# Attention with block gating and a Fourier-mixing MLP on one core: from the ninth head pair on, DMAs that transpose turn q, k and the gate mask, in place of TensorE

## The chip, the core and the metric

The kernel runs on one core of a Trainium2 chip. Its engines work side by side and meet through semaphores: TensorE (PE, matrix products and transposes by matmul, results to PSUM), VectorE (DVE), ScalarE (ACT), GpSimd (POOL) and SyncE (SP, which here issues DMAs). The metric is the device time of one execution in microseconds (us).

## The reference, cut to what matters

Inputs: q, k and v of 4 batches, 8 heads, 768 positions and 64 dimensions in float32, and two weight matrices of 512 x 2048 and 2048 x 512. First comes attention in which each query sees only some blocks of 64 keys:

```python
k_rep = k.reshape(B, H, n_blocks, block, D).mean(axis=3)      # 12 blocks of 64 keys
gate = einsum('bhsd,bhnd->bhsn', q, k_rep)                    # causal: later blocks at -1e9
sel  = top 3 blocks by gate, and the query's own block
scores = 0.125 * q @ k.T, kept where the block is selected and key <= query
attn = softmax(scores) @ v
```

Then, per batch, with x of 768 x 512 (the 8 heads side by side): `mixed = real(fft over rows and columns of x)`, `u = x + mixed`, `un = normalise(u)` along a row, `out = u + relu(un @ w_ch1) @ w_ch2`.

The gates choose blocks by comparison, so they are computed more finely than one f16 product would: in f32 for the first eight head pairs, and from f16 high and low parts for the rest.

## The kernel before, in words

Heads go in pairs, kk = 0 to 15, four per batch; the two heads of a pair are e = 0 and 1. A pair's q and k are loaded in natural layout (128 positions per partition group, six groups) as float32 (load_qk, line 211, by SP, four pairs ahead of use) into tiles of two buffers.

- stage_A (line 264) turns k (who = 1) and q (who = 0) by twelve f32 transposes on TensorE into PSUM tile `tp`. Out of `tp` for k, VectorE sums 64 keys at a time (`kr12`, line 292) and ScalarE writes f16 kI (line 311); for q, from pair SPLIT = 8 on, ScalarE writes the f16 high part `qh` scaled by 64 (line 287) and VectorE the low part `ql` (line 288), and VectorE makes high and low parts of the block sums, `krx` (lines 304 and 305). POOL copies q to its place in `qg` (cast_q, line 237).
- stage_B (line 316) makes the gates: ten matmuls on TensorE (line 323 in f32 for pairs below 8, line 331 in f16 from pair 8), then on VectorE the causal part (line 333), the sum with the low part (line 334), ten MAX8 (line 340), the comparison with the third largest (line 342) and the own block (line 348).
- stage_C (line 350) turns that mask by five f16 transposes (tile `gt`, line 354), and VectorE copies it to rows 64 to 75 of `qg` (line 357). Rows 64 to 75 of kI hold a constant of -60000 per block, so that one matmul of 76 rows gives scores and mask together.
- stage_S (line 376) makes a third of the scores of one head (PSUM tile `sc`, two buffers) and ScalarE their Exp into `ptl` (line 391); stage_AV (line 399) multiplies by v and normalises; fold (line 428 on) begins the Fourier part of the batch.

The order on PE and POOL is that in which the program emits instructions (manual_schedule, line 660); a scheduler orders the other engines. Each pair kk is a loop over six sections p = 0 to 5, and each section emits one stage_S, a piece of filler, one of the other stages, and filler again. The table USUAL places k of pair kk+2 at p = 0, stage_AV of the last pair's head 1 at p = 1, q of pair kk+2 at p = 2, stage_C of pair kk+1 at p = 3, stage_AV of head 0 at p = 4 and stage_B of pair kk+2 at p = 5; pair 6 (NORM_SLOT), in which the first batch's normalisation falls, has a table of its own. The filler is MLP work (stage_M1, line 578 for its matmuls; stage_M2, line 592) and Fourier work (stage_S1, stage_S2, stage_T) of batches whose attention is done, from a planner (class Feed) that hands out work by written-down costs: main(stage, cost) adds a stage's cost to its clock. After pair 15 the rest of the filler runs alone.

Of the kernel before, what the change touches and what calls it, by code (L numbers as in the profile page):

```python
# [19 lines left out]
def _consts_np():  # L20
# [30 lines left out]
    IndN = np.where(nn[:, None] == (s[None, :] // 64), NEG, 0.0).astype(np.float16)  # L51
    return dict(CS=CS, SS=SS, CD=CD, SDN=SDN, SDP=SDP, ident32=ident32, ident16=ident16,
                ut01=ut01, ltri=ltri, cz24=cz24, oth24=oth24, IndN=IndN)
# [65 lines left out]
def kernel(  # L119
# [65 lines left out]
    kI_t = [[const([128, S], F16, f"kI_{e}_{sl}") for sl in range(3)] for e in range(2)]  # L185
    v16_t = [const([128, 2, NST, 66], F16, f"v16_{sl}") for sl in range(4)]
    qg_t = [[const([128, S], F16, f"qg_{e}_{sl}") for sl in range(3)] for e in range(2)]
    warm = const([128, 512], F16, "warm")
    kr24_t = [const([128, 2 * NB], FP, f"kr24_{sl}") for sl in range(2)]
    krx_t = [const([128, 2, 2 * NB], F16, f"krx_{sl}") for sl in range(2)]  # L190
# [8 lines left out]
    NORM_SLOT = 6  # L199

# [32 lines left out]
    def cast_v(kk):  # L233
        P[kk]["v16"] = v16_t[kk % 4]
        nc.gpsimd.tensor_copy(out=v16_t[kk % 4][:, :, :, 0:64], in_=P[kk]["vn"])

    def cast_q(kk):
        d = P[kk]
        for e in range(2):
            nc.gpsimd.tensor_copy(out=d["qg"][e][0:64, :],  # L240
                                  in_=d["qt" if kk < SPLIT else "qh"][64 * e:64 * e + 64, :])
# [22 lines left out]
    def stage_A(kk, who, g):  # L264
        d = P[kk]
        src = d["qn"] if who == 0 else d["kn"]
        if who == 0 and g == 0:
            d["qt"] = apool.tile([128, S], FP, tag="qT32", name=f"qT32_{kk}")
            if kk >= SPLIT:
                parts = d["qt"].bitcast(F16)  # L270
                d["qh"], d["ql"] = parts[:, 0:S], parts[:, S:2 * S]
            d["qg"] = [qg_t[e][kk % 3] for e in range(2)]
        if who == 1 and g == 0:
            d["kI"] = [kI_t[e][kk % 3] for e in range(2)]
            d["kr12"] = spool.tile([128, NB], FP, tag="kr12", name=f"kr12_{kk}", bufs=2)
            d["kr24"] = kr24_t[kk % 2]
# [6 lines left out]
        if who == 0:  # L283
            if kk < SPLIT:
                (nc.scalar.copy if kk == LATE else nc.vector.tensor_copy)(out=d["qt"][:, cols], in_=flat)
            else:
                nc.scalar.activation(out=d["qh"][:, cols], in_=flat, func=AF.Copy, scale=QS)  # L287
                STT(out=d["ql"][:, cols], in0=flat, scalar=QS, in1=d["qh"][:, cols], op0=MULT, op1=SUB)  # L288
            if g == 1 and kk != LATE:
                cast_q(kk)  # L290
        else:
# [3 lines left out]
            if g == 1 and kk < SPLIT:  # L295
# [3 lines left out]
            elif g == 1:  # L299
                d["krx"] = krx_t[kk % 2]  # L300
                for e in range(2):
                    r, c = slice(64 * e, 64 * e + 64), slice(NB * e, NB * (e + 1))
                    hi, lo = d["krx"][r, 0, c], d["krx"][r, 1, c]
                    nc.vector.tensor_scalar(out=hi, in0=d["kr12"][r, :], scalar1=QS, scalar2=None, op0=MULT)
                    STT(out=lo, in0=d["kr12"][r, :], scalar=QS, in1=hi, op0=MULT, op1=SUB)
            for e in range(2):
                dst, src_ = d["kI"][e][0:64, cols], flat[64 * e:64 * e + 64]
                if kk < EARLY and g == 1 and e == 1:
                    nc.vector.tensor_copy(out=dst, in_=src_)
                else:  # L310
                    nc.scalar.copy(out=dst, in_=src_)  # L311

# [3 lines left out]
    def stage_B(kk):  # L316
# [9 lines left out]
        else:  # L326
            gps = pst([128, NG, 2, 2 * NB], f"g_{kk}")
            krx = d["krx"].rearrange("p o n -> p (o n)")
            for st in range(1, NST):
                for n, part in enumerate((d["qh"], d["ql"])):  # L330
                    nc.tensor.matmul(gps[:, st - 1, :, :].rearrange("p o n -> p (o n)"),
                                     part[:, 128 * st:128 * (st + 1)], krx, start=(n == 0), stop=(n == 1))
            nc.vector.tensor_tensor(out=gsf, in0=gps[:, :, 0, :], in1=cz24[:, 1:NST, :], op=ADD)
            nc.vector.tensor_tensor(out=gsf, in0=gps[:, :, 1, :], in1=gsf, op=ADD)
# [12 lines left out]
        else:  # L347
            STT(out=gm, in0=gm, scalar=QS, in1=oth24[:, 1:NST, :, :], op0=MULT, op1=MULT)

    def stage_C(kk):  # L350
# [5 lines left out]
        for e in range(2):  # L356
            nc.vector.tensor_copy(out=d["qg"][e][64:64 + NB, 128:S],
                                  in_=gt[32 * e:32 * e + NB].rearrange("p a c -> p (a c)"))
# [17 lines left out]
    def stage_S(kk, e, s):  # L376
        d = P[kk]
        if s == 0:
            d.setdefault("pt", {})[e] = apool.tile([128, 3 * SEC], F16, tag=f"ptl{e}",
                                                   name=f"ptl_{kk}_{e}")  # L380
# [3 lines left out]
        for (jt, a0, a1, co) in SECS[s]:  # L384
            diag = by_pe and a0 == 128 * jt
            nc.tensor.matmul(sp[:, co:co + (a1 - a0)],  # L386
                             d["kI"][e][0:76, 128 * jt:128 * (jt + 1)],
                             d["qg"][e][0:76, a0:a1], start=True, stop=not diag)
            if diag:
                nc.tensor.matmul(sp[:, co:co + 128], id16, ltri, start=False, stop=True)  # L390
        nc.scalar.activation(out=pt[:, SEC * s:SEC * (s + 1)], in_=sp[:, 0:SEC], func=AF.Exp,  # L391
                             scale=0.125 if kk < SPLIT else 0.125 / QS)
# [267 lines left out]
    with tc.manual_schedule(engines={mybir.EngineType.PE, mybir.EngineType.Pool}):  # L660
# [12 lines left out]
        for t in krx_t:  # L673
            nc.gpsimd.memset(t, 0.0)
        for t in gmp_t:
            nc.vector.memset(t, 0.0)
        for sl in range(3):
            for e in range(2):
                nc.gpsimd.dma_start(kI_t[e][sl][64:64 + NB, :], dr["IndN"].ap())
        nc.gpsimd.dma_start(ut01, dr["ut01"].ap())  # L680
        for e in range(2):
            for sl in range(3):
                nc.gpsimd.memset(qg_t[e][sl][64:64 + NB, 0:128], 0.0)
        load_v(0)
        for sl in range(4):
# [43 lines left out]
        for kk in range(NK):  # L729
            at = NORM if kk == NORM_SLOT else USUAL  # L730
            for p in range(6):
# [9 lines left out]
                if p == 1 and kk - 1 == NORM_SLOT:  # L741
                    main(stage_B, 0.35, kk + 1)
                if p == at["A1"] and kk + 2 < NK:
                    main(stage_AA, 0.7, kk + 2, 1)
# [66 lines left out]
```

## Time and profile before

| What | Value |
|---|---|
| Median of 3 runs | 333.61 us (332.26 to 334.58) |
| The profiled execution's own time | 332.94 us |
| Its span in the trace | 331.2 us, 7008 instructions |
| TensorE busy, matmuls / weight loads | 311.9 us / 202.9 us |
| VectorE, ScalarE, POOL busy | 235.7, 180.3, 84.7 us |
| Mean granted TensorE clock | 0.995 |
| Pair 8's first scores in the trace | about 106 us |
| Pair 15's last scores | about 249 us |

How to read it: matmuls are pipelined, so that a TensorE row's length overlaps the next one's, and the distance from start to start is what an item takes from TensorE. PEld is the weight load, which runs beside matmuls. Idle time of an engine matters only where the chain that ends last goes through it.

### The profile page before, as it was taken

Reading aid. Unit: us, or ns where it says so; the run is one execution under the profiler, and the core shown is the slowest. Engines: PE = TensorE matmul, PEld = TensorE weight load, DVE = VectorE, ACT = ScalarE, POOL = GpSimd, SP = SyncE. Lnnn points to the kernel's source line nnn. Section 1 sums busy time; section 2 is a strip of 40 time slices with the busy share of each in tenths; the row PEclk is TensorE's granted clock in tenths of the full one; section 3 lists DMA queues with packets and bytes.
Section 4 is the critical chain, followed back from the end, with each engine's and each line's share of the span. In section 5 each row is a group of like instructions: output and inputs, shape, how many; then the busy total and the mean of one; then the engine's idle time right before and its main releaser. Section 6 shows DMA issues by size and latency. Waiting matters only on the chain.

```text
span 331.2 us, 7008 instructions
## 1 busy us (share of the span) xinstructions
PE 311.9 (94%) x2712; PEld 202.9 (61%) x2712; DVE 235.7 (71%) x750; ACT 180.3 (54%) x276; POOL 84.7 (26%) x137
## 2 busy tenths in 40 slices
PE   8799998997889989998999989999999999999995
PEld 3567776876656666555666666656666654556442
DVE  3778889689776898999765898998457588433211
ACT  3188889789965855428486754535764302244000
POOL 8545573352481120504032030502030000000000
PEclk9999999998999999999999999999999999999999
DMA  8997999990799242425324000010000011100021
GB/s 203 230 256 186 246 136 226 155 221 7 165 188 181 54 96 75 103 70 136 99 48 97 2 0 35 32 65 32 34 2 0 2 64 63 65 1 2 32 95 63
DMA packets 85312, 31.18 MB, mean 94 GB/s; under 512 B 77736, under 2 KB 81136, under 8 KB 85280
## 3 DMA queue, kind: packets, MB, share of 16 engines
q1 hardware_dynamic: 79984, 25.88, 31.4%
q0 software_dynamic: 3552, 4.40, 8.5%
q10 hardware_dynamic: 1744, 0.46, 0.6%
q8 instruction: 21, 0.34, 0.4%
q14 instruction: 11, 0.09, 0.1%
HBM read 28.63 MB, written 6.29 MB: 105 GB/s over the span
## 4 chain that ended last, share of the span: by engine, by line
PE 73%; DVE 16%; ACT 7%; issue 1%; POOL 1%; DVEq 0%; ACTq 0%
PE ch L592 22%; PE ha L578 14%; PE sc L386 8%; PE hb L578 7%; PE av L412 5%; ACT kI L311 4%; PE g L323 3%; PE za L480 2%; DVE mx L340 2%; DVE ptl L397 2%; ACT ptl L391 2%; PE tp L279 2%; PE warm L365 2%; PE gt L354 2%; PE mx L507 2%; PE mx L508 2%
## 5 line engine op out<-in xcount | busy, mean ns | idle before, releaser
L391 ACT ACTIVATE ptl<-sc 128x896 f16<-128x896 f32 x96 | 87.3, 919 | 45.9 <-PE sc L386 36.6
L592 PE MATMUL ch<-w_sb,hT 128*128 128x512 f16 x384 | 91.4, 379 | 0.5 <-DVE qT L288 0.5
L578 PEld LDWEIGHTS <-w_sb 128*128 128x128 f16 x512 | 48.8, 97 | 38.6 <-issue 4.7
L578 PE MATMUL ha<-unT,w_sb 128*128 128x512 f16 x256 | 65.7, 378 | 1.8 <-DVE hT L583 1.4
L386 PE MATMUL sc<-qg,kI 76*128 76x512 f16 (+3 forms) x256 | 54.8, 306 | 3.6 <-ACT ptl L391 3.6
L592 PEld LDWEIGHTS <-hT 128*128 128x128 f16 x384 | 36.2, 97 | 35.1 <-issue 0.6
L581 ACT ACTIVATE hT<-ha 128x512 f16<-128x512 f32 x64 | 38.1, 597 | 33.5 <-PE ha L578 33.4
L583 DVE TENSOR_SCALAR hT<-hb 128x256 f16<-128x256 f32 x64 | 26.8, 421 | 28.9 <-PE hb L578 28.7
L578 PE MATMUL hb<-unT,w_sb 128*128 128x256 f16 x256 | 38.4, 272 | 1.1 <-ACT hT L581 0.7
L429 POOL TENSOR_TENSOR fs<-x 128x384 f16<-128x384 f16 x12 | 10.9, 909 | 105.5 <-DVE x L418 91.8
L386 PEld LDWEIGHTS <-kI 76*128 76x128 f16 x256 | 24.0, 100 | 20.3 <-issue 2.8
L311 ACT CAST kI<-tp 64x384 f16<-64x384 f32 x57 | 27.1, 475 | 14.6 <-DVE kr L292 13.6
L595 DVE TENSOR_TENSOR u<-ch,u 128x512 f32<-128x512 f32 x24 | 16.5, 685 | 19.9 <-PE ch L592 19.6
L412 PE MATMUL av<-v,ptl 128*128 128x65 f16 x672 | 26.2, 195 | 0.0
L412 PEld LDWEIGHTS <-ptl 128*128 128x128 f16 x672 | 24.8, 98 | 2.0
L292 DVE TENSOR_REDUCE kr<-tp 128x6 f32<-128x384 f32 x32 | 17.2, 551 | 7.0 <-PE tp L279 7.0
L397 DVE TENSOR_TENSOR ptl<-ptl,ut 128x384 f16<-128x384 f16 x36 | 16.0, 479 | 6.1 <-ACT ptl L391 5.7
L553 ACT ACTIVATE x<-u,nmr,rstd 128x512 f16<-128x512 f32 x12 | 8.9, 806 | 17.7 <-DVE nmr L546 17.6
L418 DVE TENSOR_TENSOR x<-av,rcp 128x384 f16<-128x384 f32 x32 | 17.8, 557 | 0.9
L390 PE MATMUL sc<-ltri,id 128*128 128x128 f16 x84 | 18.4, 219 | 0.0
L240 POOL COPY qg<-qT 64x768 f16<-64x768 f16 x16 | 14.4, 902 | 12.1 <-ACT qT L287 11.6
L520 DVE BATCH_NORM_STATS2 bst<-u 128x6 f32<-128x512 f32 x24 | 16.6, 692 | 1.2 <-ACT u L516 0.7
(112 smaller groups left out, 422.9 us busy)
## 6 DMA issues: line engine op xcount, KB each, us to landing
vn<-in_v_dram SPq DMA_DIRECT2D x32, 192.0 KB, 3.3
out_dram<-u SPq DMA_DIRECT2D x24, 256.0 KB, 2.0
kn<-in_k_dram SPq DMA_DIRECT2D x30, 192.0 KB, 3.3
qn<-in_q_dram SPq DMA_DIRECT2D x30, 192.0 KB, 3.4
w_sb<-in_moe_w_ch_dram POOLq DMA_DIRECT2D x8, 256.0 KB, 7.0
w_sb<-in_moe_w_ch_dram POOLq DMA_DIRECT2D x4, 512.0 KB, 9.5
cs_sb<-c_CS SPq DMA_DIRECT2D x1, 289.5 KB, 4.9
ss_sb<-c_SS SPq DMA_DIRECT2D x1, 289.5 KB, 5.2
```

Source lines behind the costliest of these rows:

```text
L292: nc.vector.tensor_reduce(out=d["kr12"][:, 6 * g:6 * g + 6], in_=ps.rearrange("p a (x c) -> p a x c", x=2), axis=mybir.AxisListType.X, op=ADD)
L311: nc.scalar.copy(out=dst, in_=src_)
L386: nc.tensor.matmul(sp[:, co:co + (a1 - a0)], d["kI"][e][0:76, 128 * jt:128 * (jt + 1)], d["qg"][e][0:76, a0:a1], start=True, stop=not diag)
L390: nc.tensor.matmul(sp[:, co:co + 128], id16, ltri, start=False, stop=True)
L391: nc.scalar.activation(out=pt[:, SEC * s:SEC * (s + 1)], in_=sp[:, 0:SEC], func=AF.Exp, scale=0.125 if kk < SPLIT else 0.125 / QS)
L397: nc.vector.tensor_tensor(out=dg, in0=dg, in1=um, op=MULT)
L412: nc.tensor.matmul(av[:, st, 0:65], pt[:, o:o + 128], d["v16"][:, e, jt, 0:65], start=(cnt == 0), stop=(cnt == 20))
L418: nc.vector.tensor_tensor(out=x_b[:, :, 64 * h:64 * h + 64], in0=av[:, :, 0:64], in1=rcp.to_broadcast([128, NST, 64]), op=MULT)
L578: nc.tensor.matmul(hp_, w1_sb[:, dt, 128 * it:128 * (it + 1)], unT[:, dt, c0:c1], start=(dt == 0), stop=(dt == NDT - 1))
L581: nc.scalar.activation(out=hT[:, c0:c1], in_=hp_, func=AF.Relu)
L583: nc.vector.tensor_scalar(out=hT[:, c0:c1], in0=hp_, scalar1=0.0, scalar2=None, op0=mybir.AluOpType.max)
L592: nc.tensor.matmul(cps, x["hT"][it][:, 128 * st:128 * (st + 1)], w2_sb[:, it, :], start=(it == 0), stop=(it == NIT - 1))
```

## The change

For pairs 8 to 15 stage_A and stage_C are not called. In their place `split` makes f16 high and low parts of q in natural layout (ScalarE and VectorE), side by side in `qs`, and of k in `ks` (high) and `klo` (low); transposing DMAs on SP's queue turn `qs` to `qhl` and `ks` to kI. `ks` has the -60000 constants in columns 64 to 75, so that they come along. `stage_R` adds up k's blocks on TensorE: 24 matmuls of two columns, with the high and low parts as stationary operand and a matrix of ones and zeros. Its result is split to f16 high and low parts on VectorE and copied to the upper partitions by ScalarE. stage_B multiplies `qhl` (high and low parts on 128 rows) by that, per head, writes the mask back into `qs` and a third DMA turns `qs` into `qg`. Each turn is 128 x 1536 f16. For all pairs, kI and `qg` hold the two heads in alternating blocks of 128 columns, `ptl` has one buffer per head in place of two, and `v16` three slots in place of four.

```diff
-    kI_t = [[const([128, S], F16, f"kI_{e}_{sl}") for sl in range(3)] for e in range(2)]
-    v16_t = [const([128, 2, NST, 66], F16, f"v16_{sl}") for sl in range(4)]
-    qg_t = [[const([128, S], F16, f"qg_{e}_{sl}") for sl in range(3)] for e in range(2)]
+    kI_t = [const([128, NST, 2, 128], F16, f"kI_{sl}") for sl in range(3)]
+    v16_t = [const([128, 2, NST, 66], F16, f"v16_{sl}") for sl in range(3)]
+    qg_t = [const([128, NST, 2, 128], F16, f"qg_{sl}") for sl in range(3)]
+    ks = const([128, NST, 2, 128], F16, "ks")
+    klo = const([128, NST, 2, 64], F16, "klo")
+    qs_t = [const([128, NST, 2, 128], F16, f"qs_{sl}") for sl in range(2)]
+    krs_t = [const([128, 2, 2, NB], F16, f"krs_{sl}") for sl in range(2)]
+    ind2 = const([128, 2], F16, "ind2")
...
+    def turn(dst, src):
+        nc.sync.dma_start_transpose(dst.rearrange("p s e c -> p (s e) c"),
+                                    src.rearrange("p s e c -> p (s e c)"))
+
+    def split(kk):
+        d = P[kk]
+        kn, qn = d["kn"], d["qn"]
+        d["qs"] = qs = qs_t[kk % 2]
+        d["qhl"] = apool.tile([128, S], FP, tag="qT32", name=f"qhl_{kk}").bitcast(F16).rearrange(
+            "p (s e c) -> p s e c", e=2, c=128)
+        khi, qhi = ks[:, :, :, 0:64], qs[:, :, :, 0:64]
+        nc.scalar.activation(out=qhi, in_=qn, func=AF.Copy, scale=QS)
+        STT(out=qs[:, 1:NST, :, 64:128], in0=qn[:, 1:NST, :, :], scalar=QS, in1=qhi[:, 1:NST, :, :],
+            op0=MULT, op1=SUB)
+        turn(d["qhl"], qs)
+        nc.scalar.activation(out=khi, in_=kn, func=AF.Copy, scale=QS)
+        turn(kI_t[kk % 3], ks)
+        STT(out=klo, in0=kn, scalar=QS, in1=khi, op0=MULT, op1=SUB)
+        d["kI"], d["qg"] = kI_t[kk % 3], qg_t[kk % 3]
+
+    def stage_R(kk):
+        d = P[kk]
+        d["krs"] = krs = krs_t[kk % 2]
+        rps = pst([64, 2, NB], f"r_{kk}")
+        for st in range(NST):
+            for e in range(2):
+                o = rps[:, e, 2 * st:2 * st + 2]
+                nc.tensor.matmul(o, ks[:, st, e, 0:64], ind2, start=True, stop=False)
+                nc.tensor.matmul(o, klo[:, st, e, :], ind2, start=False, stop=True)
+        hi, lo = krs[0:64, :, 0, :], krs[0:64, :, 1, :]
+        nc.vector.tensor_copy(out=hi, in_=rps)
+        nc.vector.tensor_tensor(out=lo, in0=rps, in1=hi, op=SUB)
+        nc.scalar.copy(out=krs[64:128, :, :, :], in_=krs[0:64, :, :, :])
...
             for st in range(1, NST):
-                for n, part in enumerate((d["qh"], d["ql"])):
-                    nc.tensor.matmul(gps[:, st - 1, :, :].rearrange("p o n -> p (o n)"),
-                                     part[:, 128 * st:128 * (st + 1)], krx, start=(n == 0), stop=(n == 1))
+                for e in range(2):
+                    nc.tensor.matmul(gps[:, st - 1, e, :, :].rearrange("p o n -> p (o n)"),
+                                     d["qhl"][:, st, e, :],
+                                     d["krs"][:, e, :, :].rearrange("p o n -> p (o n)"), start=True, stop=True)
...
-            STT(out=gm, in0=gm, scalar=QS, in1=oth24[:, 1:NST, :, :], op0=MULT, op1=MULT)
+            STT(out=d["qs"][:, 1:NST, :, 64:64 + NB], in0=gm,
+                scalar=QS * QS, in1=oth24[:, 1:NST, :, :], op0=MULT, op1=MULT)
+            turn(qg_t[kk % 3], d["qs"])
...
             d.setdefault("pt", {})[e] = apool.tile([128, 3 * SEC], F16, tag=f"ptl{e}",
-                                                   name=f"ptl_{kk}_{e}")
+                                                   name=f"ptl_{kk}_{e}", bufs=1)
...
-                             d["kI"][e][0:76, 128 * jt:128 * (jt + 1)],
-                             d["qg"][e][0:76, a0:a1], start=True, stop=not diag)
+                             d["kI"][0:76, jt, e, :],
+                             d["qg"][0:76, a0 // 128:a1 // 128, e, :], start=True, stop=not diag)
...
-                if p == 1 and kk - 1 == NORM_SLOT:
-                    main(stage_B, 0.35, kk + 1)
+                if p == 0 and kk - 1 == NORM_SLOT:
+                    main(stage_R, 0.4, kk + 1)
+                    main(stage_B, 0.3, kk + 1)
                 if p == at["A1"] and kk + 2 < NK:
-                    main(stage_AA, 0.7, kk + 2, 1)
-                if p == at["C"] and kk + 1 < NK:
+                    if kk + 2 < SPLIT:
+                        main(stage_AA, 0.7, kk + 2, 1)
+                    else:
+                        split(kk + 2)
+                if p == at["C"] and kk + 1 < min(SPLIT, NK):
                     main(stage_C, 0.3, kk + 1)
...
-                        main(stage_AA, 0.7, kk + 2, 0)
+                        if kk + 2 < SPLIT:
+                            main(stage_AA, 0.7, kk + 2, 0)
...
-                    main(stage_B, 1.05 if kk + 2 < SPLIT else 0.35, kk + 2)
+                    if kk + 2 >= SPLIT:
+                        main(stage_R, 0.4, kk + 2)
+                    main(stage_B, 1.05 if kk + 2 < SPLIT else 0.3, kk + 2)
...
+            if kk == 3:
+                nc.gpsimd.memset(ks[:, :, :, 64 + NB:128], 0.0)
+                for t in qs_t:
+                    nc.gpsimd.memset(t[:, 0, :, 64:128], 0.0)
+                for e in range(2):
+                    nc.sync.dma_start(ks[:, :, e, 64:64 + NB],
+                                      dr["IndT"].ap().rearrange("(st p) n -> p st n", p=128))
+                    nc.gpsimd.memset(ind2[:, e:e + 1], 0.0)
+                    nc.gpsimd.memset(ind2[64 * e:64 * e + 64, e:e + 1], 1.0)
...
-                pool_after(P[kk + 2]["qt" if kk + 2 < SPLIT else "ql"])
+                pool_after(P[kk + 2]["qt"] if kk + 2 < SPLIT else P[kk + 2]["kn"][:, 0, 0, :])
```

Since q and k are both scaled by 64 now, the Exp of these pairs has the scale 0.125 / 64^2.

## The prediction

> **What bounds the kernel now.** I read the page's busy shares first, then the busy time by stretches, then the timeline of the stretch that the change touches, then groups by line.
>
> ```profile
> PE 311.9 (94%) x2712; PEld 202.9 (61%) x2712; DVE 235.7 (71%) x750; ACT 180.3 (54%) x276; POOL 84.7 (26%) x137
> ...
> q1 hardware_dynamic: 79984, 25.88, 31.4%
> ...
> kn<-in_k_dram SPq DMA_DIRECT2D x30, 192.0 KB, 3.3
> w_sb<-in_moe_w_ch_dram POOLq DMA_DIRECT2D x8, 256.0 KB, 7.0
> ```
>
> TensorE (PE) is busy 94% of the span. The stretches (busy us of PE, weight loads, VectorE, ScalarE, POOL, then granted clock) say where:
>
> ```profile
> 170.00:190.00 20.00, 19.81 (x173) 12.95 (x172) 13.70 (x48) 14.48 (x23) 5.42 (x8) 1.00 0.18 41
> 190.00:210.00 20.00, 18.91 (x174) 12.61 (x172) 18.10 (x53) 10.93 (x18) 3.38 (x6) 1.00 0.04 14
> 210.00:230.00 20.00, 20.00 (x170) 11.68 (x167) 18.96 (x60) 9.91 (x13) 6.11 (x7) 1.00 0.14 53
> ```
>
> From 85 us on, where pairs 8 to 15 are prepared among the filler (MLP and Fourier work), PE hardly stops: between 125 and 250 us its waits add up to 2.8 us, all for VectorE. So PE time taken out there comes off the end, and a PE wait put in there goes onto it. VectorE is close behind (18.96 of 20 us), ScalarE is not. DMA is nearly idle (shares 0.04 to 0.45).
>
> ```profile
> 71.73 1.19 PE L323 MATMUL g<-kr,qT 128*128 128x24 f32 x10
> 72.77 0.27 PE L507 MATMUL mx<-cd_sb,yR 128*128 128x256 f16 x1
> ...
> 201.35 0.41 PE L331 MATMUL g<-krx,qT 128*128 128x48 f16 x10
> 201.61 0.27 PE L507 MATMUL mx<-cd_sb,yT 128*128 128x256 f16 x1
> ...
> 202.79 0.27 DVE L333 TENSOR_TENSOR gsb<-g,cz 128x120 f32<-128x120 f32 x1
> ...
> 204.15 0.82 PE L279 MATMUL tp<-id,kn 128*128 128x128 f32 x6
> 204.81 0.27 PE L507 MATMUL mx<-cd_sb,yT 128*128 128x256 f16 x1
> ...
> 213.83 0.46 PE L354 MATMUL gt<-id,gmp 128*44 128x128 f16 x5
> 214.22 0.28 PE L507 MATMUL mx<-cd_sb,yR 128*128 128x256 f16 x1
> ```
>
> Start to start is what an item costs PE, since ends overlap: six transposes of k 0.66 us (204.15 to 204.81), the mask's five 0.39 us, the ten f16 gate matmuls 0.26 us, ten f32 ones 1.04 us. And VectorE answers late: the gates end at 201.35 + 0.41 = 201.76, their first reader starts at 202.79, 1.0 us later.
>
> **What leaves PE**, per pair, eight pairs: twelve f32 transposes (0.66 for k, 0.65 for q, 210.54 to 211.19) and the mask's transposes (0.39, and some 0.09 of gap ahead: the matmul before starts at 213.53 and spaces 0.21). That is 0.66 + 0.65 + 0.48 = 1.79 us, times 8 = 14.3 us. The gate matmuls stay ten, with half the columns: taken as equal.
>
> **What PE gets: stage_R.** 24 matmuls of 2 columns, each with a weight load of 128 rows by 64 f16 columns. No row has that. Below: the f16 gates' full-width loads pass at 0.26 / 10 = 26 ns. Above: the f32 gates stream only 24 columns and still need 104 ns per 128-column load, so half the columns at that pace is 52 ns. The mask's 44-column loads (78 ns each with 128 columns streamed, where full-width f16 transposes, `unt`, take 57) lean to the slow side: I take 52 ns, 24 x 0.052 = 1.25 us per pair, 10.0 in all; at 26 ns 5.0, at 78 ns 15.0. [...]
>
> **The wait that this puts in.** stage_R and stage_B are written one right after the other with no filler between, and PE's order is the written one. B's first matmul needs krs, which takes three hand-overs after R's last matmul: VectorE copies the f16 part out of PSUM, VectorE subtracts, ScalarE copies to partitions 64 to 127. Floor: 0.18 us drain (an L331 matmul's own length), 0.04 to VectorE (av ends 199.41, L417 starts 199.45), 2 x 0.17 (the krx ops of the same size, L304 and L305's 152 to 168 ns), 0.03 to ScalarE (222.99 + 0.17, L553 starts at 223.19), 0.21 for 48 columns (L391 and L287: 0.84 ns per column over 0.17) and as little again back to PE: 0.8 us. On top come the queues: VectorE answered PE after 1.0, 0.8 (gates), 1.0 (gt), 0.04, 1.0, 0.3 (av) and 0.2 us (k), mean 0.6; but while PE stands, VectorE's backlog, which PE feeds, runs dry, so 0.4; another op slipping between the two VectorE ops (202.79 and 203.57 are such a pair, L518 between) 0.2; an Exp ahead in ScalarE 0.1. I take 1.5 us, between 0.8 and 2.6 (1.0 for VectorE, 0.7 between, an Exp 0.1 more). Times 8: 12.0 us (6.4 to 20.8). Behind the waiting matmul everything on PE queues: filler, the next scores, and so the next Exp.
>
> **VectorE, ScalarE, POOL.** VectorE loses per pair 2 x 0.550 (L292), 2 x 0.541 (L288), 2 x 0.168 and 2 x 0.237 (L304, L305), 2 x 0.483 (L357) = 3.96 us, and gains two f32 splits of 640 and 768 columns (0.82 and 0.95 by L288's 384 in 0.541 and about 1.05 ns per column) and two small ops, 0.34: 2.11. ScalarE loses 4 x 0.475 + 2 x 0.489 = 2.88 and gains 2 x 0.81 + 0.21. POOL loses 2 x 0.85. Only the 2.8 us for which PE waited for VectorE can come back from this; I take -1.0 (0 to -2).
>
> **The turning DMAs.** Three per pair, each 128 x 1536 x 2 B = 393 KB, on SP's queue. No row turns anything. Nearest: 192 KB of plain load land in 3.3 us; 2 x that, 6.6 us, if all of it scales. The w_sb loads, 256 KB in 7.0 us, would make it 10.8. By packets: 79,984 packets in 31.4% of 16 x 331.2 us are 20.8 ns each; 1,536 runs of 256 B are then 2.0 us of 16 engines, but 196,608 elements of 2 B one by one 256 us. I take some 5 us, nearest to the loads of 256 B runs. Cover: q's split is at the pair's first section, the gates at its sixth (202.90 to 219.97 in pair 13, 17 us); 0.81 + 0.82 of splitting, 2 of queues and 5 of flight fit. If the previous pair's mask turn stands ahead in SP's queue (its mask is ready some 3 us into the pair) another 5 go, which still fits. k's turn and the mask's have a pair's time. Behind a waiting turn on SP stand q/k/v loads, two pairs early, and stores that nobody awaits. So 0 us, except for pair 8: its split is at section 5 of pair 6 (79.2 us), its gates now in section 1 of pair 7 (about 85.1 where before they came at 90.65). Six us for 1.6 + 2 + 5: I put in 2 us (0 to 5).
>
> [...]
>
> **The rest.** kI and qg in blocks of 128 columns: the moving operand goes in runs of 256 B; a reordered operand of 512 columns (L515) takes 388 ns beside 378 for L592, so 0 (0 to 1). One ptl buffer: the Exp that overwrites it waits for scores that stand behind stage_AV on PE anyway, 0. Three v16 slots: POOL's cast in section 3 needs AV of section 2, and the fold ahead of it on POOL waits for the same, 0. Memsets and index loads after pair 3 on POOL (22 of 40 us busy there) and the gate of the w2 loads: 0.
>
> **Sum.** -14.3 + 10.0 + 12.0 - 1.0 + 2.0 = +8.7 us on the profiled execution's 332.94 (span 331.2, 1.7 around it): 341.6. That execution lies 0.7 below the median 333.61, so beside the median: 342.
>
> **Rivals.** (1) It gains. Place and price: R and the wait after it. The change wins where R + wait is below 1.79 us per pair, give or take the single terms. At 26 ns (5.0) and the floor (6.4): -14.3 + 5.0 + 6.4 - 1.0 = -3.9, or 330 beside the median. For it: VectorE is relieved by 1.85 us per pair and runs dry while PE stands. Against: the 104 ns and 78 ns rows. Its range is 326 to 335. (2) The turns bind. If one takes 8 us, three are 24 us against some 19 for a pair ((202.90 - 106.26) / 5 pairs): 4.7 us on seven pairs, +33, or 375; from about 6.4 us each they bind, and then SP's loads come late too. For it: the 256 KB in 7.0 us, no row against; 350 to 400. [...] (3) The turns go element by element: 24 x 256 us, over 6,000 us; only the packet arithmetic speaks for it. (4) The wait is hidden and R dear, or the reverse: no change, inside the margins of the first two.
>
> **Numbers.** Forecast 55% (its own range 334 to 354), (1) 22%, (2) 19%, (3) 4%. Changes under 1% (3.3 us) can't be told from none. Faster by over 1% (below 330.3): most of the lower part of (1), 0.15. Within 1%: the rest of (1) and the forecast's low end, 0.16. Slower: 0.69. The range 328 to 364 holds the forecast, most of (1) and the lower third of (2); out are the rest of (2), (3) and the tail of (1), about 2 in 10.
>
> **What would show it.** Right: the tp rows of PE fall by 96 and gt by 40; a group of 192 matmuls of 2 columns, starts some 50 ns apart; PE idle ahead of the g matmuls, 1 to 2 us each, released by ScalarE's krs copy; VectorE's total down by some 15 us; turns that land in about 5 us. Wrong: g waiting for a DMA instead, R at half or double its price, no idle time ahead of g, or a longer first 85 us.

## The result and the profile after

The changed kernel takes 361.2 us (median of 4 runs, 359.0 to 363.6) beside 333.66 for the kernel before on the same chip: a ratio of 1.083, 95% interval 1.075 to 1.091. That is 27.5 us slower, where 8 were forecast: the direction and the range held, the size did not. The profiled execution took 361.05 us with a span of 359.3, 28.1 over the span before. Medians, here and in the table below, are of all executions, while the ratios leave out those more than 1.5% above the fastest of their kernel.

First the page of the changed kernel: busy time of each engine, the granted TensorE clock in 40 slices of 9 us, and SP's DMA queue (packets, MB, share of 16 engines).

```profile
span 359.3 us, 7109 instructions
...
PE 321.3 (89%) x2768; PEld 203.2 (57%) x2768; DVE 229.1 (64%) x702; ACT 173.0 (48%) x252; POOL 73.1 (20%) x124
...
PEclk9999998998887968898989989899999999999998
...
q1 hardware_dynamic: 119184, 35.35, 48.6%
```

TensorE is the place to look: 9.4 us more busy (311.9 before) and 18.7 us more idle (38.0 beside 19.3), which is all of the 28.1. And the clock row (a 9 stands for 90% or more) has 8s, 7s and a 6 in the middle; the same row of the kernel before has a single 8, in its tenth slice.

What TensorE waited for from 80 to 300 us (us in total, times, the longest), and under it ScalarE's own waits there:

```profile
PE g L359 <- ACT krs L340: 12.9, 8, 2.6
PE hb L610 <- ACT hT L613: 5.6, 1, 5.6
PE ha L610 <- ACT hT L613: 3.0, 1, 3.0
PE unt L594 <- DVE x L581: 2.9, 1, 2.9
```

```profile
ACT qs L318 <- DMA qg<-qs: 17.3, 6, 8.2
ACT krs L340 <- DVE krs L339: 6.0, 4, 2.3
```

The first line is the wait that the forecast put in, once per pair and eight times. The next two, 8.6 us, were not in it. The ScalarE lines say where they come from, below.

One turn of the gates in the timeline of TensorE (start, length, line, what, how many, and in brackets the idle time ahead): the first and last matmuls of stage_R, then the gates and the filler.

```profile
139.97 0.19 PE L335 MATMUL r<-ind,ks 128*64 128x2 f16 x1
...
140.72 0.17 PE L336 MATMUL r<-ind,klo 128*64 128x2 f16 x1
142.04 0.40 PE L359 MATMUL g<-krs,qhl 128*128 128x24 f16 x10 [1.16 <-ACT krs L340]
142.29 1.82 PE L624 MATMUL ch<-w_sb,hT 128*128 128x512 f16 x4
...
148.20 1.03 PE L624 MATMUL ch<-w_sb,hT 128*128 128x512 f16 x4
```

Three things can be read here. The 24 matmuls start 33 ns apart ((140.72 - 139.97) / 23). Then TensorE stands for 1.16 us. And the same four filler matmuls that take 1.03 us at 148.20 take 1.82 at 142.29, right after the stop. The stretches of that place show the clock (length, busy us of PE, weight loads, VectorE, ScalarE, POOL, then the granted clock, the DMA share and GB/s):

```profile
138.00:142.00 4.00, 2.88 (x40) 2.04 (x38) 2.20 (x8) 2.90 (x5) 0.00 (x0) 1.00 0.00 0
142.00:146.00 4.00, 3.96 (x23) 2.07 (x23) 2.56 (x15) 0.92 (x1) 0.00 (x0) 0.57 0.90 107
146.00:150.00 4.00, 4.00 (x42) 2.42 (x40) 3.64 (x9) 0.92 (x1) 0.00 (x0) 1.00 1.12 222
```

So this stop is paid twice: 1.16 us while TensorE stands, and again over some 4 us at 0.57 of the clock. Not after each: the 1.15 us ahead of the gates at 116.25 left the clock at 1.00. In stretches of 2 us, half clock (0.50 to 0.55 in the lowest stretch of each) shows behind six of the eight gates: behind all three that waited 2.2 us or more, and behind three of the five that waited 0.9 to 1.4 us.

The unforeseen stops, first on ScalarE's timeline and then on TensorE's:

```profile
97.59 0.60 ACT L613 ACTIVATE hT<-ha 128x512 f16<-128x512 f32 x1
106.37 0.84 ACT L318 ACTIVATE qs<-qn 128x768 f16<-128x768 f32 x1 [8.19 <-DMA qg<-qs]
107.12 0.58 ACT L613 ACTIVATE hT<-ha 128x512 f16<-128x512 f32 x1
```

```profile
107.75 1.01 PE L610 MATMUL hb<-unT,w_sb 128*128 128x256 f16 x4 [5.63 <-ACT hT L613]
...
109.31 1.91 PE L610 MATMUL ha<-unT,w_sb 128*128 128x512 f16 x4
```

`qs` has two buffers, so the f16 copy of q of pair 10 (L318) needs the mask turn of pair 8 to have read the same buffer. The scheduler had placed that copy early in ScalarE's order. It waits 8.19 us there, and behind it stands the Relu of the MLP (L613), which needs no DMA and for which TensorE stands 5.63 us. On SP's own timeline the mask turn of pair 8 (the row at 100.03) was late because two turns of pair 9 stood ahead of it:

```profile
88.81 6.59 SPq L308 DMA_TRANSPOSE qhl<-qs  x1
95.58 3.72 SPq L308 DMA_TRANSPOSE kI<-ks  x1
...
100.03 1.75 SPq L308 DMA_TRANSPOSE qg<-qs  x1
...
187.80 1.43 SPq L308 DMA_TRANSPOSE qg<-qs  x1
```

In the median a turn holds SP for 1.4 us (as in the row at 187.80); at 88.81, with two loads of the second weights (from 87.67 us) and two of k (from 87.75 us) issued just ahead, one held it for 6.59.

### The profile page after: what moved, and what is told of

It reads as the page before. It is cut to its first block, busy times and chain, and to the rows that moved or that the text cites. A ratio compares the mean times of both kernels' runs of the same rounds, so it can differ in the third digit from the quotient of the medians.

```text
span 359.3 us, 7109 instructions
## 1 busy us (share of the span) xinstructions
PE 321.3 (89%) x2768; PEld 203.2 (57%) x2768; DVE 229.1 (64%) x702; ACT 173.0 (48%) x252; POOL 73.1 (20%) x124
## 3 DMA queue, kind: packets, MB, share of 16 engines
q1 hardware_dynamic: 119184, 35.35, 48.6%
## 4 chain that ended last, share of the span: by engine, by line
PE 70%; DVE 12%; ACT 7%; DMA 7%; issue 2%; POOL 0%; SPq 0%; ACTq 0%; DVEq 0%
PE ch L624 23%; PE ha L610 13%; PE sc L418 8%; PE hb L610 7%; PE av L444 4%; DMA qg<-qs 4%; ACT ptl L423 3%; PE za L512 2%; PE g L352 2%; DVE ptl L429 2%; PE ya L516 2%; ACT kI L305 2%; DMA cz<-c_cz 1%; PE mx L539 1%; PE mx L540 1%
## 5 line engine op out<-in xcount | busy, mean ns | idle before, releaser
L624 PE MATMUL ch<-w_sb,hT 128*128 128x512 f16 x384 | 93.6, 388 | 0.0
L610 PEld LDWEIGHTS <-w_sb 128*128 128x128 f16 x512 | 51.5, 102 | 50.6 <-issue 18.8
L610 PE MATMUL ha<-unT,w_sb 128*128 128x512 f16 x256 | 71.7, 406 | 3.4 <-ACT hT L613 3.0
L418 PE MATMUL sc<-qg,kI 76*128 76x512 f16 (+3 forms) x256 | 56.9, 317 | 3.4 <-ACT ptl L423 3.4
L624 PEld LDWEIGHTS <-hT 128*128 128x128 f16 x384 | 37.0, 99 | 37.1 <-issue 2.9
L613 ACT ACTIVATE hT<-ha 128x512 f16<-128x512 f32 x64 | 38.0, 596 | 40.0 <-PE ha L610 40.0
L615 DVE TENSOR_SCALAR hT<-hb 128x256 f16<-128x256 f32 x64 | 26.4, 420 | 38.4 <-PE hb L610 38.2
L610 PE MATMUL hb<-unT,w_sb 128*128 128x256 f16 x256 | 41.4, 288 | 6.6 <-ACT hT L613 5.6
L418 PEld LDWEIGHTS <-kI 76*128 76x128 f16 x256 | 24.7, 103 | 22.1 <-issue 5.1
L627 DVE TENSOR_TENSOR u<-ch,u 128x512 f32<-128x512 f32 x24 | 16.5, 686 | 22.5 <-PE ch L624 22.2
L429 DVE TENSOR_TENSOR ptl<-ptl,ut 128x384 f16<-128x384 f16 x36 | 17.1, 514 | 4.3 <-ACT ptl L423 4.3
L422 PE MATMUL sc<-ltri,id 128*128 128x128 f16 x84 | 18.7, 223 | 0.0
L243 POOL CAST v<-vn 128x768 f16<-128x768 f32 x16 | 14.6, 915 | 12.4 <-DMA vn<-in_v_dram 9.2
L319 DVE SCALAR_TENSOR_TENSOR qs<-qn,qs 128x640 f16<-128x640 f32 x8 | 7.7, 967 | 13.2 <-ACT qs L318 13.0
L550 DVE TENSOR_TENSOR u<-mx,x 128x512 f32<-128x512 f32 x18 | 12.3, 681 | 6.1 <-PE mx L540 5.8
```

Of the source, the lines that this page charges most:

```text
L418: nc.tensor.matmul(sp[:, co:co + (a1 - a0)], d["kI"][0:76, jt, e, :], d["qg"][0:76, a0 // 128:a1 // 128, e, :], start=True, stop=not diag)
L429: nc.vector.tensor_tensor(out=dg, in0=dg, in1=um, op=MULT)
L610: nc.tensor.matmul(hp_, w1_sb[:, dt, 128 * it:128 * (it + 1)], unT[:, dt, c0:c1], start=(dt == 0), stop=(dt == NDT - 1))
L613: nc.scalar.activation(out=hT[:, c0:c1], in_=hp_, func=AF.Relu)
L615: nc.vector.tensor_scalar(out=hT[:, c0:c1], in0=hp_, scalar1=0.0, scalar2=None, op0=mybir.AluOpType.max)
L624: nc.tensor.matmul(cps, x["hT"][it][:, 128 * st:128 * (st + 1)], w2_sb[:, it, :], start=(it == 0), stop=(it == NIT - 1))
```

## The experiments

Theory A: the loss is TensorE's stops (12.9 us for `krs`, 8.6 behind ScalarE's wait for the mask turn) and the half clock behind them. Rival B: the DMA engines bound the kernel once 24 turns are on them. Rival C: the lower clock only mirrors the waits and costs nothing by itself. All ratios are to the kernel before, measured on the same chip. The table stands ahead, since the readings go back to it; all kernels from the change on have the same 2768 matmuls (but for those with added ones), so that a difference of busy time is one of clock, but for some 0.2 us per stop, by which the last matmul ahead of it no longer overlaps the next (an estimate from the kernel before: a `ch` matmul of 512 columns lasts 379 ns, and four take 1.03 us, so that one starts some 0.22 us after the other).

| Kernel | Median, us | Ratio (95%) | Span of the profile | PE busy | PE idle |
|---|---|---|---|---|---|
| before | 333.66 | 1 | 331.2 | 311.9 | 19.3 |
| after | 361.2 | 1.083 (1.075 to 1.091) | 359.3 | 321.3 | 38.0 |
| e1_apart | 342.85 | 1.025 (1.018 to 1.031) | 340.8 | 309.9 | 30.9 |
| e2_anchor | 355.81 | 1.067 (1.064 to 1.071) | 354.7 | 315.8 | 38.9 |
| e3_warm (+56 matmuls) | 355.86 | 1.069 (1.064 to 1.074) | 354.6 | 324.2 | 30.4 |
| e4_both | 334.95 | 1.002 (0.998 to 1.007) | 337.4 | 312.7 | 24.7 |
| e5_free | 331.73 | 0.995 (0.993 to 0.997) | 330.0 | 307.8 | 22.2 |
| e6_w2 | 327.25 | 0.981 (0.977 to 0.985) | 326.4 | 307.4 | 19.0 |
| e7_anchor | 348.75 | 1.045 (1.041 to 1.049) | 344.8 | 314.6 | 30.2 |
| e8_late | 331.6 | 0.994 (0.992 to 0.997) | 330.7 | 308.6 | 22.1 |
| e9_start | 327.33 | 0.982 (0.979 to 0.985) | 328.5 | 307.7 | 20.8 |
| e10_stop4 (+12) | 358.47 | 1.063 (1.058 to 1.068) | 357.9 | 320.7 | 37.2 |
| e11_stop2 (+12) | 346.3 | 1.038 (1.035 to 1.041) | 341.9 | 309.8 | 32.1 |

The profiled executions of e4_both, e9_start and e10_stop4 (339.2, 330.3 and 360.1 us) ran above their medians, that of e11_stop2 below its own.

### e1_apart: the sums one section ahead of the gates

```diff
+                if p == at["B"] - 1 and p < 5 and SPLIT <= kk + 2 < NK:
+                    main(stage_R, 0.4, kk + 2)
...
                 if p == at["B"] and kk + 2 < NK:
-                    if kk + 2 >= SPLIT:
-                        main(stage_R, 0.4, kk + 2)
```

For pair 8 the sums come in the first section of pair 7 and the gates in the second.

> stage_R goes one section ahead of stage_B (pair 8: section 1 and 2 of pair 7), nothing else changes. Theory A (stops of TensorE and the half clock that follows each): the 12.9 us that the gate matmuls waited for ScalarE's krs copy fall below 3 us, and the clock that was lost after these stops, some 10 us (six stretches of about 8 us that each lose 1.7), comes back too: 338 us (334 to 344) against 361. Rival B (the DMAs are the bound, their share was above 1.0 between 60 and 130 us and each turn adds 2.9 us of all 16 engines): the gates then wait for the turned q instead, 353 us or more. Rival C (the granted clock only mirrors the waits and costs nothing of its own): 12.9 us less, 348.

Measured: 342.85 us, 18.4 less than the changed kernel. No gate waits for `krs` any more, and the busy time fell by 11.4 us at the same count of matmuls: the order of two calls was worth 7.1 us of idle time and 11.4 of clock. It is 5 us above A's 338, though inside its range. The idle time fell by 7.1 us where A had 10 to 13: ScalarE's wait for the mask turn, 8.6 us before, now makes TensorE stand for 9.4 us in one piece, and the waits for VectorE's `hT` (L615) grew from 0.7 to 5.6 us:

```profile
PE hb L610 <- ACT hT L613: 9.4, 1, 9.4
...
PE hb L610 <- DVE hT L615: 2.1, 1, 2.1
PE za L512 <- DVE hT L615: 1.7, 1, 1.7
```

B's 353 and C's 348 fall.

### e2_anchor and e7_anchor: the copy of q tied to its place on ScalarE

```diff
-        nc.scalar.activation(out=pt[:, SEC * s:SEC * (s + 1)], in_=sp[:, 0:SEC], func=AF.Exp,
+        X["exp"] = nc.scalar.activation(out=pt[:, SEC * s:SEC * (s + 1)], in_=sp[:, 0:SEC], func=AF.Exp,
...
-        nc.scalar.activation(out=qhi, in_=qn, func=AF.Copy, scale=QS)
+        with tc.issue_after(X["exp"].ins):
+            nc.scalar.activation(out=qhi, in_=qn, func=AF.Copy, scale=QS)
```

In e7_anchor the tie holds from the eleventh pair on only (`if kk >= 10 else nullcontext()`).

> ScalarE's first step of split (the f16 high part of q) is tied behind the Exp that the program emitted last, so that it keeps its written place in ScalarE's order in place of one up to a section or more earlier, where it stood waiting for the mask turn of two pairs before. Theory A: ScalarE's 17.3 us of waiting for the mask turns fall below 4, the 8.6 us that TensorE waited for hT behind it and some 5 us of lost clock go, the gates' wait stays at about 13: 347 us (343 to 352). Rival B (DMAs are the bound): q's turn comes too late now and the gates wait for it: 357 or more. Rival C: 352.

> The tie of the copy of q from the eleventh pair on alone, with the sums of the blocks left right ahead of the gates, as in the changed kernel. Theory A: of the changed kernel's 361 us go the two stops that ScalarE's wait for the mask's turn made (5.6 and 3.0 us) and the half clock behind them (about 5 us): 347 us (343 to 352); the wait of some 12 us for the sums stays. Rival D (the stops of ScalarE and those for the sums are one loss, shared: who waits at one place needs not wait at the other): 355 us or more.

The first missed (355.81) and the second hit (348.75 for 347 forecast). From 80 us on TensorE waits for this in e2_anchor and then in e7_anchor:

```profile
PE g L360 <- ACT krs L341: 12.1, 7, 2.6
PE g L360 <- DMA qhl<-qs: 11.1, 1, 11.1
```

```profile
PE g L360 <- ACT krs L341: 12.9, 8, 2.6
PE unt L595 <- DVE x L582: 2.9, 1, 2.9
```

In both, no matmul waits behind ScalarE's wait for the mask turn. In e2_anchor the tie also held pair 8's copy, whose buffer had been free all along; its turn came late and cost 11.1 us at one gate. That is the kind of wait that B named, but for this one pair alone. With that pair and the next left free, the tie is worth 12.4 us by the medians and 14.5 by the spans (7.8 of idle time, 6.7 of clock). And the wait for `krs` is 12.9 us still, to the tenth: the two losses are separate, and rival D falls.

### e3_warm: useless matmuls in the wait

```diff
                     main(stage_R, 0.4, kk + 1)
+                    stage_W(7)
...
                         main(stage_R, 0.4, kk + 2)
+                        stage_W(7)
```

stage_W multiplies a constant tile by itself, 512 columns each, and nothing reads the result.

> Seven matmuls of 512 columns on a constant tile (some 1.5 us, their result is not used) stand between stage_R and stage_B, so that TensorE is busy while it waits for krs. Nothing is computed sooner. Theory A: the gates' wait falls from 12.9 to 4 us or less while 12 us of useless work come in, and the clock stays up: 351 us (347 to 356). Rival C (no cost of the clock itself): 361, within 3.

Measured: 355.86, 5.3 us less than the changed kernel although TensorE got some 12 us of useless work (56 matmuls of 512 columns, 0.215 us each by the four `ch` matmuls from 148.20 to 149.06). Its busy time rose by 2.9 only. So the matmuls that were there before took 9 us less, and that is clock: C falls here most directly. The granted clock rose from 0.940 to 0.965. It is 5 us above A's 351: ScalarE's wait for the mask turn stayed and made TensorE stand for 8.1 us in one piece, and 2.3 us of the wait for `krs` were left.

### e4_both, e5_free, e6_w2: both cures, and then what is left

e4_both joins e1_apart and e2_anchor; e5_free has the tie of e7_anchor in place of that of e2_anchor; e6_w2 spreads the second weight matrix:

```diff
-            if kk in (6, 7):
+            if kk in (5, 6, 7, 8):
                 pool_after(P[kk + 2]["qt"] if kk + 2 < SPLIT else P[kk + 2]["kn"][:, 0, 0, :])
-                load_w2(2 * kk - 12)
-                load_w2(2 * kk - 11)
+                load_w2(kk - 5)
```

> The edits of the first two runs together. Theory A: the terms add up, 361 - 13 - 10 - 9 - 5 = 325 us (319 to 333), below the 333.7 of the kernel before, since the transposes that left TensorE were worth 14 us and stage_R takes 0.76 us per pair. Rival B: 345 or more, with waits for the turns in place of those removed. Rival C: 340.

> As the run that had both cures (the sums of the blocks one section ahead of the gates, and the ScalarE copy of q tied behind the Exp emitted before it), but the tie now holds only from the eleventh pair on: for the ninth and the tenth the tile that this copy fills has not been used, and the tie only made it late. Theory A (the loss is TensorE's stops and the half clock behind each): the two waits left there, 7.5 us for the turn of q of the ninth pair and 3.7 us for its mask, go, and with them some 2 us of the low clock of 100 to 130 us: 322 us (317 to 328), some 11 under the kernel before. Rival B (the DMA engines, full from 85 to 130 us, are the bound there and only the place of the wait moves): 331 us or more.

> The same, with the four loads of the second weight matrix (512 KB each) spread over the ends of the pairs 5, 6, 7 and 8, one at each, in place of two at the end of 6 and two at the end of 7: less stands on the DMA engines when the first turns are issued, and no byte is taken away. Theory A: TensorE's waits there are short already, so 0 to 3 us under the run before it: 320 us (316 to 325). Rival B: at least 6 us under it, since the turns of the ninth and the tenth pair land earlier by what the two loads took from them.

e4_both came to 334.95, level with the kernel before and 10 above forecast: pair 8's late copy again (7.5 us at its gates and 3.7 at its successor's scores). e5_free came to 331.73, also 10 above A's forecast and where B had put it (331 or more). Its one long wait is a DMA, 5.60 us for the tenth pair's mask, and the stretch around it runs at 0.66 of the clock:

```profile
112.77 0.91 PE L419 MATMUL sc<-qg,kI 76*128 76x512 f16 x3 [5.60 <-DMA qg<-qs]
```

```profile
110.00:120.00 10.00, 7.23 (x39) 3.79 (x38) 1.62 (x4) 4.19 (x6) 0.00 (x0) 0.66 1.28 208
120.00:130.00 10.00, 10.00 (x124) 7.28 (x121) 8.90 (x23) 7.08 (x12) 1.87 (x3) 1.00 0.72 145
130.00:150.00 20.00, 20.00 (x193) 12.36 (x191) 18.16 (x50) 9.13 (x12) 2.82 (x3) 1.00 0.85 158
```

The DMA share (the last number but one) reads 1.28 there and TensorE waits; from 120 us on it is lower and TensorE never stops. So B is right for this one stretch. Spreading the second weights, without one byte less, took 4.5 us more off (327.25); that wait fell to 2.2 us. A allowed for 3, B asked for 6: both in part. e6_w2 beats the kernel before by 1.9% (1.5 to 2.3), and from 120 to 250 us its TensorE is busy 130.00 of 130 us at full clock.

### e8_late and e9_start: the loss before pair 7

In the changed kernel pair 7's scores start 3.4 us late (88.11 for 84.75), before anything new runs on TensorE. Two edits, each on the best kernel then at hand:

```diff
-            if kk == 3:
+            if kk == 5:
                 nc.gpsimd.memset(ks[:, :, :, 64 + NB:128], 0.0)
```

```diff
-        for sl in range(3):
+        def ind_rows(sl):
             for e in range(2):
                 nc.gpsimd.dma_start(kI_t[sl][64:64 + NB, :, e, :],
...
+        ind_rows(0)
...
         cast_v(0)
+        ind_rows(1)
+        ind_rows(2)
         load_qk(2)
```

> The first of these runs, with the block that fills the tables of the new path (two loads of 18 KB in pieces of 24 bytes, memsets on GpSimd) moved from the end of pair 3 to the end of pair 5. In the changed kernel 2.8 us are lost between the gates of pair 5 and those of pair 6, where this block runs. If the block causes them: 2 to 3 us under the first run, 319 us. If the loss is one of another order of VectorE's and ScalarE's work there: the same within 1 us, 322 us.

> The best run so far (327.25 us: sums one section ahead, the tie from the eleventh pair on, second weights' loads spread) with one edit at the start: of the six loads that fill the constant rows of the three key buffers, which the change cut from pieces of 1,536 bytes into pieces of 256, the four for the second and third buffer are issued after the first cast of v instead of ahead of everything. In the traces the first scores start at 16.66 us before and at 17.9 to 18.5 in every changed kernel, since the loads of k, q and the gates' table land later. If those pieces cause it: 1.3 us come back, 326.0 us (325 to 327). If something else at the start does: 327.2, the same.

Both changed nothing (331.6 beside 331.73, and 327.33 beside 327.25): pair 7's scores still start at 88.31 and 89.03 us, and in e9_start the first scores of all at 18.09. Neither the tables' block nor the cut constant rows are the cause. What is seen is a start 1.3 us later (17.94 for 16.66) and a low clock in the first Fourier stretch: twelve `za` matmuls take 1.78 us where they took 1.16 before. TensorE's wait for the normalised x of the first batch also grew, from 1.56 us (at 78.20) to 2.85 (at 83.25). The causes of the three stay open.

### e10_stop4 and e11_stop2: what a stop costs by itself

```diff
+                if p == at["B"] and 10 <= kk + 2 < NK:
+                    sps = pst([128, 64], f"stop_{kk}")
+                    nc.tensor.matmul(sps, warm[:, 0:128], warm[:, 0:64], start=True, stop=True)
+                    for i in range(4):
+                        nc.gpsimd.memset(warm, 0.0)
+                    nc.tensor.matmul(sps, warm[:, 0:128], warm[:, 0:64], start=True, stop=True)
```

The base is e6_w2; e11_stop2 has `range(2)`.

> The best run so far, in which TensorE neither stops nor loses its clock from 130 to 250 us, with an artificial stop in each of the last six pairs, where the gates' turn comes: a 64-column matmul on a constant tile, four memsets of that tile on GpSimd (about 0.52 us each, estimated from 0.74 for 768 columns), and another such matmul that waits for them. Nothing else waits for these, and no other work is added or moved. Six stops of some 2.4 us. Theory A (behind each stop stands half clock, worth some 1.3 us, from 10 us lost at eight junctions in the changed kernel): 6 x (2.4 + 1.3) = +22, so 349 us (344 to 354), and a granted clock of 0.5 to 0.9 in the 4 us behind each. Theory C (the clock of the records only mirrors the wait): 6 x 2.45 = +15, so 342 (339 to 343.5). Rival E (the stop is made up by the work that waits behind it, since other engines run ahead): 335 or less.

> The same with two memsets, so six stops of some 1.3 us. Theory A as it stands (a stop this short already halves the clock, as at the junctions of the changed kernel where the sums waited 1.2 to 2.6 us): 6 x (1.3 + 1.3) = +16, so 343 us (339 to 346). Rival F (a stop has to be longer by itself, and in the changed kernel it was the 24 narrow matmuls of the sums right ahead of the wait, with the idle time on both sides, that dropped the clock): 6 x 1.35 = +8, 335 us (333.5 to 337), granted clock 1.00 behind the stops.

Both medians are higher than any of the expectations, in part for a reason that I built in: POOL works in written order, so the last load of the second weights stood behind the memsets and TensorE waited for it, 2.5 us in one profile and 6.1 in the other. The stretches from 170 to 230 us hold only the artificial stops. First e10_stop4, then e11_stop2:

```profile
170.00:190.00 20.00, 17.54 (x161) 10.51 (x160) 10.62 (x36) 10.07 (x15) 4.89 (x9) 0.91 0.71 150
190.00:210.00 20.00, 17.60 (x163) 10.89 (x161) 11.30 (x38) 11.18 (x17) 3.16 (x7) 0.91 0.40 79
210.00:230.00 20.00, 17.54 (x146) 10.62 (x145) 13.62 (x40) 9.02 (x14) 3.86 (x7) 0.83 0.25 46
```

```profile
170.00:190.00 20.00, 18.71 (x179) 11.79 (x177) 12.51 (x40) 12.45 (x19) 4.79 (x7) 1.00 0.64 133
190.00:210.00 20.00, 18.77 (x191) 12.55 (x189) 15.07 (x47) 12.52 (x20) 2.93 (x5) 1.00 0.32 61
210.00:230.00 20.00, 18.70 (x170) 10.97 (x168) 17.76 (x50) 7.71 (x11) 3.73 (x5) 1.00 0.44 100
```

Each stretch has one stop, of 2.4 to 2.5 us above and 1.3 below. Above, the matmuls behind a stop run at half speed, four of 512 columns in 1.91 us (1.03 at full clock in the row at 148.20 above):

```profile
200.88 0.20 PE L807 MATMUL stop<-warm 128*128 128x64 f16 x1 [2.40 <-POOL warm L806]
...
201.63 1.91 PE L611 MATMUL ha<-unT,w_sb 128*128 128x512 f16 x4
```

Five of the six long stops were followed by half clock (that at 155.8 us was not), none of the five short ones from 150 us on. That count is of one execution, the profiled one (span 357.9 us, mean clock 0.952): the six executions of e10_stop4 ran from 350.0 us at 0.966 to 361.4 us at 0.943, so the number of stops that cost clock seems to change from one to the next. The spans close to about 1 us: e10_stop4 is 31.5 us over e6_w2, of which 14.7 are the stops, 2.5 the weights' wait and 13.2 longer busy time, the twelve added matmuls among it; e11_stop2 is 15.5 over it, of which 7.6 are stops, 6.1 the weights' wait and 2.4 busy time, with its low clock behind the 6.1 (0.83 from 130 to 150 us). So A's mechanism holds for a stop of 2.4 us (some 2 us of clock on top where the clock fell), and the first half of rival F for one of 1.3. That the changed kernel lost its clock behind three waits of 0.86, 1.16 and 1.20 us, and kept it behind two of 1.15 and 1.43, fits F's second half, that the 0.76 us of two-column matmuls ahead of the wait count as part of the stop, but doesn't show it; no run here took these apart.

## Why the prediction was wrong: point by point

The spans differ by 28.1 us, and that is -14.3 (work gone, at the prediction's price) + 6.1 (stage_R) + 17.6 (clock: the 9.4 us of longer busy time, plus the 8.2 that it should have fallen) + 12.9 (gates waiting) + 8.6 (behind ScalarE) - 2.8 (the rest of the idle time). The 3.4 us lost before pair 7 lie in these terms, not beside them. The forecast's sum was +8.7.

- **Work that leaves TensorE, -14.3.** The instructions went: `tp` from 192 matmuls to 96, `gt` from 80 to 40. That the price was about right is borne out by the best kernel: TensorE is busy 4.5 us less in e6_w2 than before, and its mean clock of 0.984 over 326.4 us is 5.2 us short of full speed where 0.995 over 331.2 is 1.7 short. Without those 3.5 us it would be 8.0 less, beside 14.3 - 6.1 = 8.2.
- **stage_R, 10.0: too high.** Measured 0.76 us per pair, 6.1 in all. The prediction chose 52 ns between its ends of 26 and 78, led by f32 loads and by 44-column transposes. The measured step is 31 to 33 ns: a 64-column f16 load passes nearly as fast as a full one, and the lower end was the row to go by (the f16 gates, 26 ns).
- **The wait for `krs`, 12.0.** Right: 12.9, between 0.9 and 2.6 each, through the queues named. The longest, 2.59 us at 163.26, has on VectorE the next pair's `klo` between the two small ops, because `klo` has one buffer and stage_R had just freed it:

```profile
161.61 0.15 DVE L338 CAST krs<-r 64x24 f16<-64x24 f32 x1
161.73 0.18 DVE L553 BATCH_NORM_AGGREGATE stat<-bst 128x2 f32<-128x6 f32 x1
161.83 0.96 DVE L324 SCALAR_TENSOR_TENSOR klo<-kn,ks 128x768 f16<-128x768 f32 x1
...
162.78 0.17 DVE L339 TENSOR_TENSOR krs<-r,krs 64x24 f16<-64x24 f32 x1
```

- **The step that failed: "a PE wait put in there goes onto it".** The prediction priced a wait at its length. The clock was 1.00 in the stretches it showed, stretches in which TensorE hardly stops, and the sum has no term for a lower one. The missing 17.6 us are the largest term of all; 13.9 of them are gone in e6_w2 with the same matmuls. The granted clock gives the same size: a mean of 0.940 over 359.3 us is 21.6 us short of full speed, 19.9 more than before, and some 2.5 of these passed while TensorE stood. The trace of the kernel before had the sign in it, outside the stretches that the prediction read: one stop of 1.56 us, and half clock behind it.

```profile
78.20 0.40 PE L562 MATMUL unt<-id,x 128*128 128x128 f16 x4 [1.56 <-DVE x L549]
```

```profile
80.00:84.00 4.00, 4.00 (x43) 3.54 (x42) 3.47 (x11) 3.33 (x8) 1.79 (x2) 0.61 0.34 79
```

The runs show how long that loss lasts and how short a stop can bring it: four of the five half-clock stretches behind the stops of e10_stop4 last some 3.4 us and one 6.8 (worked out from the granted clock, as 0.89, 0.50 and 0.76 in the 2 us stretches from 176 to 182 us). A stop of 2.4 us with nothing else was enough five times in six, and 1.16 us behind stage_R at 142 us.
- **The second step that failed: "k's turn and the mask's have a pair's time ... So 0 us".** For TensorE they had. But it is the mask's turn that also frees `qs`, on which ScalarE's copy for the pair after next waits, and nobody asked what stands behind that copy: the MLP's Relu, and so TensorE, 8.6 us. e7_anchor took this away alone.
- **The turns' own time, some 5 us.** Right: they land in 4.3 (q), 4.1 (k) and 3.7 us (mask) in the median, and rivals (2) and (3) fall as they were put. What the prediction missed is that the turns share the DMA engines: SP's queue went from 31.4% of 331.2 us to 48.6% of 359.3, or 2.9 us of all sixteen engines per turn (2.0 forecast), and between 85 and 120 us that was too much at once (e6_w2: 4.5 us).
- **Pair 8's turn, +2.0.** In the changed kernel its gates waited for no turn: the scheduler had put the copy of its q at 71.39 us and not at 79.2, and its turn was issued at 73.86. The delay came with its mask turn, by ScalarE.
- **VectorE, -1.0.** The idle time outside the named waits fell by 2.8 us, to which this belongs. VectorE's busy time fell by 6.6 us, not by 15: the rows that the change touches fell by 13.1 (31.1 out, 18.0 in). Of the rest, 2.5 us came back in rows that it does not touch, for a reason left open, and 4.0 are overlap: rows that follow each other closely overlap a little and count once in the busy time, and fewer do so now (the rows add up to 256.2 us before and 245.6 after, for 235.7 and 229.1 of busy time).
- **The first 85 us, 0.** Wrong by 3.4, with the cause open (e8_late, e9_start).

Rival (1), that it gains, was right about the kernel and wrong about this version of it: R + wait was 2.4 us per pair and not under 1.79. With both waits taken out by order alone it wins by 0.5% (e5_free), and by 1.9% once the weights' loads make room (e6_w2).

## What to carry to other kernels

Where TensorE is busy without a break, price a new wait at its length plus the clock that may be lost behind it (some 2 us behind a stop of 2.4 us in e10_stop4, in five cases of six), and put a producer of TensorE's own (here the block sums) a section ahead of its consumer, so that three hand-overs have work to hide under (18.4 us in e1_apart). For every DMA that reads a buffer, ask which engine next writes that buffer, in what order its queue stands, and what unrelated work is behind that write (8.6 us of TensorE here). When new DMAs come in, look at what else is on the DMA engines at that time, and move the loads that have slack (4.5 us in e6_w2).

## What the runs showed of the hardware that I had not expected

- A stop of TensorE of 2.4 us was followed by half clock in five cases of six (one execution; some 3.4 us of it in four, 6.8 in one), one of 1.3 us in none of five; the price was about 2 us where the clock fell. Behind stage_R's two-column matmuls, waits of 0.86 to 1.20 us were enough in three cases of four, and one of 1.43 us was not. Useless matmuls in the gap were cheaper than the gap (e3_warm: 12 us of work put in, 5.3 us gained).
- Matmuls of two columns with a 64-column f16 weight load pass at 31 to 33 ns.
- A transposing DMA of 393 KB from SBUF to SBUF lands in 3.7 us at best and holds SP's queue for 1.4 us in the median, but for 6.6 us where two loads of the weights and two of k had been issued just ahead, and everything behind it in that queue waited as long.
